# A new pace table for attention's blocks beside the units of a Strassen-like product: more in the first and last unit of each round, fewer in the units between

## The chip, the cores and the metric

The kernel runs on one core of one Trainium2 chip, as one program in one launch. The metric is the device time of that program in microseconds (us). Five engines run side by side, each through its own list of instructions in order: TensorE (PE, matrix products), VectorE (DVE), ScalarE (ACT), GpSimd (POOL) and SyncE (SP). SP issues nearly all DMA transfers, POOL the rest. An engine that must wait for another holds up everything that stands behind the waiting instruction on its own list.

## What is computed

Two independent layers, whose outputs of 2048 x 1024 float32 each are set side by side:

```python
def _A_ref(x, wqkv, wo):
    H = 32; Dh = D // H; W = 256
    qkv = (x @ wqkv).reshape(B, S, 3, H, Dh).transpose(2, 0, 3, 1, 4)
    q, k, v = qkv[0], qkv[1], qkv[2]
    scores = jnp.einsum("bhqd,bhkd->bhqk", q, k) * (Dh ** -0.5)
    mask = (idx[:, None] - idx[None, :] >= 0) & (idx[:, None] - idx[None, :] < W)
    p = _softmax(jnp.where(mask[None, None], scores, -1e9), axis=-1)
    o = jnp.einsum("bhqk,bhkd->bhqd", p, v)
    return o.transpose(0, 2, 1, 3).reshape(B, S, D) @ wo

def _B_ref(x, dft_seq_re, dft_seq_im, dft_hid_re, dft_hid_im):
    a = jnp.einsum("bsd,ed->bse", x, dft_hid_re)
    b = jnp.einsum("bsd,ed->bse", x, dft_hid_im)
    return jnp.einsum("ts,bse->bte", dft_seq_re, a) - jnp.einsum("ts,bse->bte", dft_seq_im, b)

return jnp.concatenate([_A_ref(...), _B_ref(...)], axis=-1)
```

S is 2048, D is 1024. The first is attention of 32 heads in a sliding window of 256 keys; the second is four plain products with cosine and sine matrices that come in as inputs.

## The kernel before

Every float32 operand is split into a float16 high part and a float16 rest, and each product is made of three products of parts. The work comes in four stretches.

*Projections* (to 566 us). A list `order` names 96 pieces of q, k and v, each 24 products of 128 x 512. Between them preparations run for what follows.

*Units* (566 to 1570 us). The second layer's products, 48 units of the helper `seven`, each a 2 x 2 block product with seven multiplications in place of eight: seven positions of twelve products, 84 in all. They use three PSUM banks, a, b and c, in the sequence a b a c a b a; at each position's end ACT or DVE empties the bank just filled (lines 1032, 1034 and 1066), and PE comes back to it one or two positions later. A round has twelve units: four of kind "x" (names `p1_...`, product with the hidden matrix), whose left operand was split beforehand and is loaded ready-made (`x_left`: `un_a`, `un_b`, `un_c` and a part in `reg`), and eight of kind "c" (`p2_...`, product with the sequence matrix), for each of which `u_step` splits a raw tile one unit ahead on ACT and DVE. So during the last unit of a round and the first three of the next no raw tile is split, while the ready-made operands are loaded (for the first unit of a round during the last one of the round before). There are four rounds; units are counted from 0, so rounds begin at units 0, 12, 24 and 36. A "c" unit makes two output tiles. In round 0 SP stores them; from round 1 on they are added to what lies in memory by four accumulating stores per unit, issued by POOL in the unit after (`store`, line 1125).

*Attention* runs beside the projections and the units, as a Python generator that puts its steps between their products. One block is a pair of heads by 128 queries; there are 256. A block's steps: on PE its scores into `s` and `far` (`s_step`); on DVE a masked copy (line 254) and the row maximum (256); on ACT the bias (259), two exponentials (266) and the float16 copy `hl` (269); on DVE the rest of that copy (270); on SP a transposing DMA from `hl` into `t` (272); on POOL two triangular selections (`z_step`, 284 and 286), which stand behind a `mark` that follows a later block's bias; six blocks later on PE the product with v (`v_step`) and on DVE its sum (318). After four blocks `o_step` normalizes, and SP transposes the result (`ot`, line 335) and stores it into `ots` (354). Tile `hl` has three buffers, `s` three banks, `t` six. A block's q, k and v are loaded by SP for four blocks at a time (`qk` line 222, `vt` line 228), about three blocks ahead.

*Tail* (from 1570 us): the output projection, eight units `po0` to `po7`, with nothing of attention left.

How many blocks stand beside which products is set by `tick`: after every four products it adds `4 * rate` to an account, and each whole point is half a block. The rate of a unit is twice a number from the tables `FIRST` (for the four "x" units of a round) and `SECOND` (for its eight "c" units), over 84, so the number is the unit's blocks. Whatever the tables leave of the 256 blocks goes to the projections: `early` is the rest, spread with the weights `EARLY`. At the fifth "c" unit of round 3 everything left is issued at once.

PE's products keep the order in which they are written, and so do ACT's and DVE's instructions where an explicit dependence says so; elsewhere the framework's scheduler orders the instructions of each engine by its own estimate.

The lines that the tables act on:

```python
def tick(n):
    ...
    acc[0] += n * rate[0]
    while acc[0] >= 1.0:
...
early = (NG * NCH * 2 * QB + LAG - in_units) / sum(EARLY.values())
...
rate[0] = 2 * early * EARLY.get(n, 0.85) / 24
...
rate[0] = 2 * ((FIRST if kind == "x" else SECOND)[2 * p + c] + (0,) * 8)[i] / 84
```

Of the kernel before, what the change touches and what calls it, by code (L numbers as in the profile page):

```python
# [53 lines left out]
def fused_kernel(ctx: ExitStack, tc: tile.TileContext, xa, wqk, wv, wo, xb, wd, cs, out):  # L54
# [342 lines left out]
    def at(n, f, *args):  # L397
# [2 lines left out]

    START = 24
    LAST = 4
    FIRST = ((6.6, 4.8, 4.4, 0.6), (4.4, 4.8, 4.8, 0.6), (3.7, 4.9, 4.9, 0.6), (3.7, 5.2, 4.9, 0.6))
    SECOND = ((2.4, 5.0, 5.0, 5.0, 5.0, 5.0, 5.0, 6.2), (2.0, 4.6, 4.6, 4.6, 4.6, 4.2, 4.2, 3.9),
              (2.0, 4.6, 4.6, 4.6, 4.6, 5.0, 5.0, 3.9), (2.0, 4.6, 4.6, 4.6))
    EARLY = {n: (1.0, 0.75, 0.9, 1.05, 1.15, 1.15)[(n - START) // 12] for n in range(START, len(order))}
    in_units = sum(sum(a) for a in FIRST + SECOND) - 0.4 * SECOND[3][LAST - 1]
    early = (NG * NCH * 2 * QB + LAG - in_units) / sum(EARLY.values())
# [677 lines left out]
    with tc.tile_pool(name="pb", bufs=1) as pb:  # L1086
# [45 lines left out]
        for n, (kind, p, c, i) in enumerate(units):  # L1132
            rate[0] = 2 * ((FIRST if kind == "x" else SECOND)[2 * p + c] + (0,) * 8)[i] / 84
            if kind == "x":
# [109 lines left out]
```

## Time and profile before

| | us |
|---|---|
| three runs | 1717.8, 1725.38, 1728.74 |
| their median | 1725.38 |
| the profiled execution | 1720.77 |
| its span, from the first to the last instruction | 1719.0 |
| idle time of PE within the span (1719.0 less 1697.8 busy) | 21.2 |
| DVE busy in the span | 1301.7 |
| ACT busy in the span | 1170.4 |

The granted clock of PE is 0.999 of its full value over the span. A product's own duration in the profile is longer than the time to the next one's start, since products overlap in the array; busy time counts the union. A row of the grouped view names line, engine, operation and operands, then busy time, mean nanoseconds of one, and the idle time of its engine just before it with what ended it. A row of the timeline has the start, the time, and in square brackets the idle time before it and its releaser. A row of the view by stretch gives, for each engine, the busy time and the number of instructions, then the granted clock, the DMA share (the mean busy share of 16 DMA engines; transfers that overlap on one engine both count, so it can pass 1) and GB/s. "SPq" are the DMA instructions on SP's list.

### The profile page before, as it was taken

The page shows a single profiled execution, that of the slowest core. Times are in us where ns is not written, and L with a number is a line of the kernel's source. Part 1 is how long each engine was busy: PE and PEld are TensorE (multiplying, and loading weights), DVE is VectorE, ACT ScalarE, POOL GpSimd, SP SyncE. Part 2 cuts the span into 40 slices and gives each one's busy share as a digit, 9 for nine tenths or more (in the row PEclk, how much of TensorE's full clock was granted, in tenths as well). Part 3 has the DMA queues.
Part 4 walks back from the last instruction along what each step waited for, and adds up shares of the span by engine and source line. Part 5 has one row for each costly group of instructions (what it writes and reads, how often), then busy time and mean ns, then how long its engine had stood idle before and what let it go on. Part 6 is the DMA issues. An engine that isn't in the chain of part 4 may idle for free.

```text
span 1719.0 us, 30875 instructions
## 1 busy us (share of the span) xinstructions
PE 1697.8 (99%) x10999; PEld 852.8 (50%) x10999; DVE 1301.7 (76%) x2225; ACT 1170.4 (68%) x2035; POOL 574.5 (33%) x874
## 2 busy tenths in 40 slices
PE   9999999999999999999999999999999999999999
PEld 4444555554555554555544545555545545444444
DVE  6847788887987788887688786688886688687542
ACT  4466666676876787887787876678876687563322
POOL 0001322444434432444423564433555424411000
PEclk9999999999999999999999999999999999999999
DMA  9747999999998985887998999986999976875431
GB/s 348 246 136 243 252 292 285 270 262 294 250 243 198 212 221 126 206 191 192 235 252 221 189 168 173 224 209 119 193 170 182 214 203 130 169 186 115 119 98 74
DMA packets 469899, 348.63 MB, mean 203 GB/s; under 512 B 376944, under 2 KB 409968, under 8 KB 468848
## 3 DMA queue, kind: packets, MB, share of 16 engines
q1 hardware_dynamic: 462064, 321.48, 74.8%
q0 software_dynamic: 7680, 25.17, 9.2%
q8 instruction: 86, 1.41, 0.3%
q14 instruction: 69, 0.57, 0.1%
HBM read 166.99 MB, written 106.17 MB: 159 GB/s over the span
## 4 chain that ended last, share of the span: by engine, by line
PE 71%; DVE 11%; ACT 7%; DMA 5%; issue 4%; POOL 2%; SPq 0%; DVEq 0%; ACTq 0%; POOLq 0%
PE p_a L114 17%; PE pv L114 13%; PE pk L114 9%; PE p_b L114 8%; PE pq L114 8%; PE po_a L114 5%; PE p_c L114 4%; PE po_b L114 2%; DMA t<-hl 2%; PE s L114 2%; DVE reg L834 1%; DVE hl L270 1%; DVE y L1034 1%; PE po_c L114 1%; ACT s L266 1%
## 5 line engine op out<-in xcount | busy, mean ns | idle before, releaser
L266 ACT ACTIVATE s<-s,bias,escs 128x256 f32<-128x256 f32 (+1 forms) x512 | 270.0, 528 | 11.7
L284 POOL TENSOR_SCALAR_AFFINE_SELECT z<-t 128x512 f16<-128x512 f16 x224 | 185.3, 835 | 189.4 <-PE pv L114 143.0
L270 DVE TENSOR_TENSOR hl<-s,hl 128x512 f16<-128x512 f32 (+1 forms) x256 | 170.2, 665 | 60.9 <-ACT hl L269 60.0
L259 ACT ACTIVATE bias<-mx,pshift,escs 128x2 f32<-128x2 f32 x256 | 98.1, 383 | 164.1 <-DVE mx L256 163.7
L114 PEld LDWEIGHTS <-reg 128*128 128x128 f16 x1344 | 129.1, 98 | 141.5
L286 POOL TENSOR_SCALAR_AFFINE_SELECT t<-t 128x512 f16<-128x512 f16 x224 | 182.9, 825 | 11.4
L114 PE MATMUL p_a<-reg,un_c 128*128 128x512 f16 x768 | 182.9, 381 | 1.1 <-ACT y L1032 0.9
L114 PE MATMUL pk<-reg,wu_k 128*128 128x512 f16 x768 | 174.4, 379 | 0.0
L256 DVE TENSOR_REDUCE mx<-s 128x2 f32<-128x512 f32 (+1 forms) x256 | 170.9, 668 | 3.4
L114 PE MATMUL pv<-reg,reg 128*128 128x512 f16 x768 | 172.7, 379 | 0.0
L114 PEld LDWEIGHTS <-un_c 128*128 128x128 f16 x1152 | 110.3, 98 | 124.7 <-issue 6.5
L263 POOL TENSOR_SCALAR mark<-bias 128x1 f32<-128x1 f32 x128 | 53.0, 414 | 353.3 <-ACT bias L259 352.9
L114 PEld LDWEIGHTS <-un_a 128*128 128x128 f16 x1152 | 109.8, 97 | 122.1 <-issue 6.7
L114 PEld LDWEIGHTS <-un_b 128*128 128x128 f16 x1152 | 110.1, 97 | 121.4 <-issue 5.5
L269 ACT ACTIVATE hl<-s 128x512 f16<-128x512 f32 (+1 forms) x256 | 148.8, 581 | 17.0 <-DMA t<-hl 11.4
L114 PE MATMUL pq<-reg,wu_q 128*128 128x512 f16 x672 | 151.3, 379 | 0.8 <-DVE reg L121 0.5
L114 PE MATMUL p_a<-reg,un_a 128*128 128x512 f16 x576 | 136.2, 379 | 4.4 <-DVE y L1034 4.2
L114 PE MATMUL p_b<-reg,un_b 128*128 128x512 f16 x576 | 136.7, 379 | 1.9 <-DVE reg L834 1.9
L114 PE MATMUL p_a<-reg,un_b 128*128 128x512 f16 x576 | 136.4, 379 | 1.8 <-DVE y L1034 1.6
L114 PE MATMUL p_c<-reg,un_a 128*128 128x512 f16 x576 | 136.5, 379 | 0.0
L254 DVE COPY_PREDICATED s<-upper,far 128x256 f32<-128x256 uint32 x224 | 94.5, 422 | 49.4 <-PE s L114 47.9
L114 PEld LDWEIGHTS <-qk 96*128 96x128 f16 x1056 | 87.9, 97 | 65.7 <-issue 2.6
(208 smaller groups left out, 3154.2 us busy)
## 6 DMA issues: line engine op xcount, KB each, us to landing
raw_u<-in_cs_dram SPq DMA_DIRECT2D x64, 512.0 KB, 4.9
qk<-qk SPq DMA_DIRECT2D x64, 384.0 KB, 4.9
out_dram<-y POOLq DMA_DIRECT2D x72, 256.0 KB, 6.2
raw_wd<-in_wd_dram SPq DMA_DIRECT2D x24, 512.0 KB, 5.3
vs<-yv SPq DMA_DIRECT2D x32, 264.0 KB, 4.4
vt<-vs SPq DMA_DIRECT2D x64, 132.0 KB, 4.4
raw_wo<-in_wo_dram SPq DMA_DIRECT2D x16, 512.0 KB, 7.4
qk<-yq SPq DMA_DIRECT2D x32, 256.0 KB, 3.2
```

The costliest lines, as they stand in the source:

```text
L114: fixed[:] = [nc.tensor.matmul(*args, **kwargs)]
L254: nc.vector.copy_predicated(s[:, :, P:], upper2, d["far"] if nb == 3 else never2)
L256: nc.vector.tensor_reduce(mx, sv, axis=AX.X, op=ALU.max, negate=True)
L259: nc.scalar.activation(bias, mx, AF.Identity, bias=pshift, scale=es)
L263: marks[:] = [nc.gpsimd.tensor_scalar(mark, bias[:, 0:1], 1.0, None, op0=ALU.mult)]
L266: nc.scalar.activation(sv[:, h], sv[:, h], AF.Exp, bias=bias[:, h:h + 1], scale=es)
L269: nc.scalar.activation(hi, sv, AF.Copy)
L270: behind[:] = [nc.vector.tensor_tensor(lo, sv, hi, op=ALU.subtract)]
L284: nc.gpsimd.affine_select(out=z, in_=pk, compare_op=ALU.is_gt, fill=0.0, base=0, pattern=[[0, 4], [-1, P]], channel_multiplier=1)
L286: nc.gpsimd.affine_select(out=pk, in_=pk, compare_op=ALU.is_ge, fill=0.0, base=0, pattern=[[0, 4], [1, P]], channel_multiplier=-1)
L834: nc.vector.tensor_tensor(lo, src, hi, op=ALU.subtract)
L1034: slice(None), [nc.vector.scalar_tensor_tensor(y, ps, f, y, op0=ALU.mult, op1=ALU.add)])
```

## The change

Two tables of numbers are replaced; nothing else is touched.

```diff
-    FIRST = ((6.6, 4.8, 4.4, 0.6), (4.4, 4.8, 4.8, 0.6), (3.7, 4.9, 4.9, 0.6), (3.7, 5.2, 4.9, 0.6))
-    SECOND = ((2.4, 5.0, 5.0, 5.0, 5.0, 5.0, 5.0, 6.2), (2.0, 4.6, 4.6, 4.6, 4.6, 4.2, 4.2, 3.9),
-              (2.0, 4.6, 4.6, 4.6, 4.6, 5.0, 5.0, 3.9), (2.0, 4.6, 4.6, 4.6))
+    FIRST = ((7.4, 4.8, 4.4, 0.6), (6.6, 4.7, 4.6, 0.6), (6.4, 4.8, 4.7, 0.6), (6.4, 5.0, 4.7, 0.6))
+    SECOND = ((1.6, 4.3, 4.3, 4.3, 4.3, 4.3, 4.3, 6.6), (1.6, 3.9, 3.9, 3.9, 3.9, 3.9, 3.9, 6.4),
+              (1.6, 3.9, 3.9, 3.9, 3.9, 3.9, 3.9, 6.4), (1.6, 4.2, 4.2, 4.2))
```

Counted in the built order by the blocks whose scores PE makes in each unit, before and now:

| round | first unit | next four | six in the middle | last unit |
|---|---|---|---|---|
| 0 (units 0 to 11) | 7, now 8 | 12, now 11 | 30, now 26 | 6, now 7 |
| 1 (12 to 23) | 5, now 6 | 12, now 12 | 27, now 23 | 3, now 7 |
| 2 (24 to 35) | 4, now 6 | 13, now 12 | 28, now 23 | 4, now 6 |
| 3 (36 to 47) | 4, now 7 | 12, now 12 | 7, now 6 | 0, now 0 |

The projections get 84 blocks for 82. The sum is 256 in both.

The first place is SP's list at the border of rounds 1 and 2, from the loads of unit 24's last operands (`un24_b`, `un24_c`) to unit 25's first (`un25_a`). In the names, `t_181` is block 181's transposed tile. Before:

```order
L272 DMA_TRANSPOSE t_181_13349<-hl_181_13346 128x8x128
L786 DMA un24_b_13400<-xs_60 128x2048
L786 DMA un24_c_13436<-xs_60 128x2048
L272 DMA_TRANSPOSE t_182_13393<-hl_182_13390 128x8x128
L781 DMA reg1_83<-xs_60 128x1024
L786 DMA un25_a_13521<-xs_60 128x2048
```

Now:

```order
L786 DMA un24_b_13326<-xs_60 128x2048
L272 DMA_TRANSPOSE t_179_13285<-hl_179_13282 128x8x128
L228 DMA vt_5_1_2_13403<-vs_58 128x4x132
L786 DMA un24_c_13394<-xs_60 128x2048
L272 DMA_TRANSPOSE t_180_13319<-hl_180_13316 128x8x128
L335 DMA_TRANSPOSE ot_5_0_3_13364<-ohl_5_0_3_13361 128x4x128
L222 DMA qk_5_1_2_13401<-qk_57 96x2048
L781 DMA reg1_83<-xs_60 128x1024
L354 DMA ots_59<-ot_5_0_3_13364 128x512
L272 DMA_TRANSPOSE t_181_13391<-hl_181_13388 128x8x128
L786 DMA un25_a_13502<-xs_60 128x2048
```

Between the load of `un24_b` and that of `un25_a` stood one block's transpose; now three stand there, with a transpose and a store of an `ot`.

The second place is DVE's list in unit 32, in the middle of round 2, from the first instruction after the last step on the raw tile of unit 33 to the instruction that empties bank a of unit 32 (line 1034, `p2_32_a`). Before:

```order
L254 COPY_PREDICATED s_216_15754<-upper_90,far_1026 128x2x128
L121 TENSOR_REDUCE top1_u34_15747<-top_u34_15668 128x1
L256 TENSOR_REDUCE mx_216_15762<-s_216_15754 128x2
L270 TENSOR_TENSOR hl_215_15718<-s_215_15704,hl_215_15718 128x512
L318 TENSOR_REDUCE o_6_1_0_15676<-pv_210_15789 128x132
L121 SCALAR_TENSOR_TENSOR un33_c_15782<-raw_u33_1_15117,sc_u33_15622,un33_c_15782 128x1024
L327 RECIPROCAL rs_6_1_0_15815<-o_6_1_0_15676 128x8
L1034 SCALAR_TENSOR_TENSOR y2_6765<-p2_32_a_15632,fu32_15348,y2_6765 128x512
```

Now:

```order
L254 COPY_PREDICATED s_215_15742<-upper_90,far_1026 128x2x128
L256 TENSOR_REDUCE mx_215_15748<-s_215_15742 128x2
L121 SCALAR_TENSOR_TENSOR un33_c_15762<-raw_u33_1_15134,sc_u33_15599,un33_c_15762 128x1024
L270 TENSOR_TENSOR hl_214_15689<-s_214_15677,hl_214_15689 128x512
L1034 SCALAR_TENSOR_TENSOR y2_6835<-p2_32_a_15609,fu32_15331,y2_6835 128x512
```

Ahead of the emptying of the bank stood five instructions of attention (lines 254, 256, 270, 318 and 327, of blocks 215 and 216 and of an earlier block's sum); now three do.

The third place is SP's list in the projections, at the load of q and k for blocks 48 to 51 (`qk_1_1_0`). Before:

```order
L272 DMA_TRANSPOSE t_43_4285<-hl_43_4282 128x8x128
L887 DMA qk_57<-yq4_3_4390 128x512
L272 DMA_TRANSPOSE t_44_4332<-hl_44_4329 128x8x128
L886 DMA qk_57<-yq4_3_4390 128x2x512
L335 DMA_TRANSPOSE ot_1_0_1_4374<-ohl_1_0_1_4371 128x4x128
L222 DMA qk_1_1_0_4446<-qk_57 96x2048
```

Now:

```order
L272 DMA_TRANSPOSE t_43_4247<-hl_43_4244 128x8x128
L886 DMA qk_57<-yq4_2_4355 128x2x512
L222 DMA qk_1_1_0_4401<-qk_57 96x2048
L648 DMA wx_114<-in_wd_dram 128x1024
L939 DMA wds_61<-wx_114 256x1x1024
L335 DMA_TRANSPOSE ot_1_0_1_4347<-ohl_1_0_1_4344 128x4x128
L272 DMA_TRANSPOSE t_44_4297<-hl_44_4294 128x8x128
```

The load stood behind block 44's transpose and that of `ot_1_0_1`; now it stands ahead of both.

## Prediction

> **What bounds the kernel now.** I read the head of the page first, to see which engine fills the span.
>
> ```profile
> span 1719.0 us, 30875 instructions
> PE 1697.8 (99%) x10999; PEld 852.8 (50%) x10999; DVE 1301.7 (76%) x2225; ACT 1170.4 (68%) x2035; POOL 574.5 (33%) x874
> ```
>
> TensorE (PE) is busy all but 21.2 us. The change moves attention's blocks and neither adds nor removes a product, so those 21.2 us, with what slow products cost, are all that can be won. The second view is the busy time by stretch, cut at the first product of a unit: units 1 to 4, the middle of round 0 (units 5 to 10), units 11 and 12, then the same four kinds again: 13 to 16, middle 17 to 22, 23 and 24, 25 to 28, middle 29 to 34, 35 and 36, 37 to 40.
>
> ```profile
> core 0: us, PE busy (x) PEld busy (x) DVE busy (x) ACT busy (x) POOL busy (x), PEclk, DMA share, GB/s
> 588.50:670.00 81.50, 81.00 (x536) 40.66 (x533) 71.65 (x122) 63.97 (x116) 25.82 (x37) 1.00 0.70 173
> 670.00:798.20 128.20, 128.12 (x969) 67.85 (x968) 111.02 (x207) 110.14 (x202) 58.49 (x85) 1.00 0.81 189
> 798.20:841.80 43.60, 43.60 (x352) 23.50 (x351) 26.12 (x48) 30.06 (x59) 15.61 (x29) 1.00 1.04 245
> 841.80:924.50 82.70, 80.72 (x521) 40.26 (x519) 70.70 (x125) 64.13 (x114) 26.08 (x34) 1.00 0.93 256
> 924.50:1056.70 132.20, 128.50 (x921) 66.43 (x920) 106.59 (x187) 101.75 (x188) 72.48 (x99) 0.99 0.98 169
> 1056.70:1097.60 40.90, 40.90 (x285) 20.89 (x283) 20.02 (x36) 22.39 (x43) 16.82 (x26) 1.00 1.09 217
> 1097.60:1178.90 81.30, 80.83 (x526) 40.62 (x525) 70.83 (x124) 64.55 (x116) 27.94 (x37) 1.00 0.77 177
> 1178.90:1309.20 130.30, 127.60 (x952) 67.07 (x950) 109.94 (x196) 105.50 (x192) 75.82 (x101) 1.00 0.98 174
> 1309.20:1350.40 41.20, 41.20 (x289) 21.16 (x288) 20.84 (x36) 24.39 (x48) 19.39 (x31) 1.00 1.04 213
> 1350.40:1434.30 83.90, 81.64 (x547) 40.86 (x545) 72.50 (x124) 64.96 (x116) 25.37 (x36) 1.00 0.79 180
> ```
>
> Length less PE's busy time is its idle time. The middles of rounds 1 and 2 lose 3.70 and 2.70 us; the middle of round 0, with more blocks but no accumulating stores, 0.08. The stretches of units 1 to 4, 13 to 16, 25 to 28 and 37 to 40 lose 0.50, 1.98, 0.47 and 2.26. The last and first units lose nothing, and there VectorE (DVE) is busy 49% and 51% in rounds 1 to 3, against 81% and 84% in the middles. But their DMA share, 1.09 and 1.04, is the highest of all. Third, I looked at what ends the two longest idle times of the middles.
>
> ```profile
> 1257.58 2.75 PE L114 MATMUL p_b<-reg 128*128 128x512 f16 x12
> 1262.04 1.24 PE L114 MATMUL p_a<-reg,un_b 128*128 128x512 f16 x5 [1.59 <-DVE y L1034]
> ...
> 1023.98 0.22 PE L114 MATMUL far<-qk 96*128 96x128 f16 x1 [1.38 <-DVE s L254]
> 1025.33 4.44 PE L114 MATMUL p_a<-reg,un_c 128*128 128x512 f16 x12 [0.85 <-ACT y L1032]
> ...
> 1022.27 0.60 ACT L269 ACTIVATE hl<-s 128x512 f16<-128x512 f32 x1 [5.17 <-DMA t<-hl]
> 1257.45 0.60 ACT L269 ACTIVATE hl<-s 128x512 f16<-128x512 f32 x1 [4.02 <-DMA t<-hl]
> ...
> 1242.82 4.74 SPq L272 DMA_TRANSPOSE t<-hl  x1
> 1247.65 1.22 SPq L335 DMA_TRANSPOSE ot<-ohl  x1
> 1257.79 0.33 SPq L354 DMA_DIRECT2D ots<-ot  x1
> 1258.22 3.94 SPq L272 DMA_TRANSPOSE t<-hl  x3
> ```
>
> PE waits for a PSUM bank that DVE or ScalarE (ACT) empties, but both were late because ACT stood 5.17 and 4.02 us in front of a copy into `hl`. That tile has three buffers, and one is free when its transposing DMA has landed. At 1247.65 SyncE (SP) issued the transpose of `ot`, and the store of it in the next row went out only at 1257.79, once `ot` had landed; three `t` transposes stood behind it. So the bound is PE, and what breaks it are late transposes, by way of `hl`.
>
> **Part 1: fewer blocks in the middles.** By the order, the middles of rounds 1 and 2 go from 27 and 28 blocks to 23 each, that of round 0 from 30 to 26. One block costs ACT and DVE this much:
>
> ```profile
> L266 ACT ACTIVATE s<-s,bias,escs 128x256 f32<-128x256 f32 (+1 forms) x512 | 270.0, 528 | 11.7
> L270 DVE TENSOR_TENSOR hl<-s,hl 128x512 f16<-128x512 f32 (+1 forms) x256 | 170.2, 665 | 60.9 <-ACT hl L269 60.0
> L259 ACT ACTIVATE bias<-mx,pshift,escs 128x2 f32<-128x2 f32 x256 | 98.1, 383 | 164.1 <-DVE mx L256 163.7
> L256 DVE TENSOR_REDUCE mx<-s 128x2 f32<-128x512 f32 (+1 forms) x256 | 170.9, 668 | 3.4
> L269 ACT ACTIVATE hl<-s 128x512 f16<-128x512 f32 (+1 forms) x256 | 148.8, 581 | 17.0 <-DMA t<-hl 11.4
> L254 DVE COPY_PREDICATED s<-upper,far 128x256 f32<-128x256 uint32 x224 | 94.5, 422 | 49.4 <-PE s L114 47.9
> ```
>
> DVE 0.665 + 0.668 + 0.422 = 1.76 us, ACT 2 x 0.528 + 0.383 + 0.581 = 2.02 us. Five blocks fewer in a middle of 130 us take 8.8 us from DVE, from 84% to about 80%, and the three buffers of `hl` last one fifth longer. Idle time to win: 3.70 + 2.70 = 6.4 us. To it comes a slow stretch: the twelve products at 1025.33 took 4.44 us where twelve at 1257.58 took 2.75, so 1.69 us more, right behind two idle times of 1.38 and 0.85. Together 8.1 us. It can win at most this, and lose a little if the new order makes other collisions: -8.1 to +2. The cause is a DMA's landing, which thinner blocks ease without removing; I take 70%, -5.7. The middle of round 0 has 0.08 to give: nothing.
>
> The Trainium skill (TensorE: Matmul & The Clock Gate, section "Why this matters for your kernels") asks for no idle gaps of over about 3 us if throughput isn't to drop. By that rule the 1.69 us aren't the work of the two gaps, and the sum would be 0.7 x 6.4 = 4.5 us won in place of 5.7. The row speaks against it here, with gaps of half that size and less, and I go by the row.
>
> **Part 2: more blocks in the last and first units.** The pair 23 and 24 goes from 7 blocks to 13, 35 and 36 from 8 to 13, 11 and 12 from 11 to 13. PE's time for them only moves. Engines: six blocks more give DVE 20.02 + 6 x 1.76 = 30.6 us and ACT 22.39 + 6 x 2.02 = 34.5, in a pair that PE's own work makes longer: 168 products of (2.75 - 0.38) / 11 = 0.215 us (0.38 is one product's own time) are 36.2 us, and with 11 blocks the pair took 43.6, so 0.67 us a block and 44.9 us with 13. That is 68% and 77%. POOL's part of a block:
>
> ```profile
> L284 POOL TENSOR_SCALAR_AFFINE_SELECT z<-t 128x512 f16<-128x512 f16 x224 | 185.3, 835 | 189.4 <-PE pv L114 143.0
> L286 POOL TENSOR_SCALAR_AFFINE_SELECT t<-t 128x512 f16<-128x512 f16 x224 | 182.9, 825 | 11.4
> ```
>
> Six times 0.835 + 0.825 on 16.82 are 26.8 us, 60%; the four stores that POOL issues in each of these units stand behind marks, which come closer together now. So these three engines hide it. Each block also brings a transpose to SP's queue, and every fourth block two loads, the transpose of `ot` and its store, between the loads of the next unit's weights. The transposes may not be hidden:
>
> ```profile
> L272 SPq DMA_TRANSPOSE t<-hl x11: 1237/1522/2924, 800.7 to 837.0; - x11
> DMA to landing us min/median/max: 3.0/5.2/7.5
> ...
> L272 SPq DMA_TRANSPOSE t<-hl x8: 1319/1616/4258, 1058.7 to 1094.9; - x8
> DMA to landing us min/median/max: 4.2/7.0/8.5
> ...
> L272 SPq DMA_TRANSPOSE t<-hl x8: 1237/1682/3722, 1310.8 to 1348.3; - x8
> DMA to landing us min/median/max: 2.8/7.5/9.7
> ```
>
> These are the pairs 11/12 (no POOL stores), 23/24 and 35/36. A buffer of `hl` is held for 0.58 (ACT) + 0.67 (DVE) + a place in SP's queue (about one transpose, 1.6) + 7.0 to 7.5 to the landing, some 10 us. Three buffers give one block each 3.3 us. The new pace is 44.9 / 13 = 3.45 us, and in a last unit of seven blocks (84 x 0.215 + 7 x 0.67) / 7 = 3.25. So the loop is just at its limit there, where before (pace 40.9 / 7 = 5.8) it had room. If the medians hold, only the late ones cost: a landing of 9.7 makes the loop 12.6, 2.9 us past three blocks at 3.25. I take one such wait per pair, less half a us that the banks give: 2.5 us each, +5 in all for two pairs. Lower end 0, as in the pair 11/12 with eleven blocks and no idle time. Upper end: at 10 us the loop takes 12.85 us, 4.28 a block, 0.83 over the pace; 13 blocks, two pairs: +22, and +3.4 if each pair meets a slow stretch of 1.69. The pair 11/12 gets two blocks more at a landing of 5.2: nothing, up to +2.
>
> **Part 3: units 1 to 4, 13 to 16, 25 to 28, 37 to 40.** They keep 12, 12, 13, 12 blocks as 11, 12, 12, 12. Their idle 5.2 us stand in units in which round products, not blocks, load DVE: I take 0, between -3 and +3.
>
> **Part 4: before the units.** Two blocks more, 84 for 82, are 3.5 us of DVE, spread over all the projections: nothing. One wait there is on the path:
>
> ```profile
> L114 PE MATMUL s<-qk 96*128 96x256 f16 (+1 forms) x512 | 105.7, 258 | 1.7 <-DMA qk<-qk 1.7
> ```
>
> It falls on block 48, whose load stands behind the `ot` transpose and block 44's on SP. In the new order it stands ahead of both. I take -1.5, between -1.7 and +1 (another load may be late next).
>
> **Sum.** -5.7 + 5 + 0 - 1.5 = -2.2 us. The profiled execution took 1720.8 us (span 1719.0 and 1.8 around it), so 1718.6 by its own measure. The median of the three runs, 1725.4, lies 4.6 above it: 1723.2 by that. The single execution and the three runs bear about equally on what a new median will be: I say 1721.
>
> **Rivals.** First, the other sign: the `hl` loop becomes the bound of the two pairs. For it speaks the DMA share, at its peak there already and about to take five and six more blocks' transposes; against it, that the pair 11/12 ran eleven blocks without idle time, though without POOL's stores. It decides when the landing's median in the pairs passes 7.8 us, since then (0.58 + 0.67 + 1.6 + 7.8) / 3 = 3.55 is 0.1 over the pace, and 26 x 0.1 with the two late ones of part 2 is the 7.2 us that parts 1 and 4 win. At 10 us: +25.4 - 7.2 = +18, 1739 by its own measure, 1744 by the median. Second, all waits of the middles and block 48 go and no new one comes: -8.1 - 1.7, and -3 from part 3: 1708 by its own measure, 1713 by the median. For it speaks that the middle of round 0 lost 0.08 us with five blocks a unit; against it, that this middle has no accumulating stores. Third, the waits merely change their places, since stores and loads stay where they are and an `ot` that lands late stops SP at any pace: 1721 to 1725.
>
> **Chances and range.** Forecast (own time within 8 us of the profiled one) 0.55; the loop as bound 0.24, half of it beyond +1%; all waits gone 0.13; only moved 0.08. About 1% is what a measurement of this kernel can tell from no change: 1708 and 1743 from the median. Faster than that needs the second rival and a low measurement: 0.06. Slower: 0.12. Within: 0.82. The range reaches from just past the second rival's end to the middle of the first one's, 1707 to 1740; the forecast's own is 1713 to 1731.
>
> **What would show it.** Part 1: idle time of PE in units 17 to 22 and 29 to 34 down from 6.4 to about 2 us, and ACT's waits for `t<-hl` there shorter. Part 2: landing of `t` near 7 to 8 us in units 23/24 and 35/36, one or two waits of ACT for `hl` there, DVE at about 70%. Part 4: no wait for `qk` near 413 us. I am wrong if PE idles over 10 us in the two pairs, or if the middles keep their 6 us though they have fewer blocks.

## The result, and the profile after

The changed kernel takes 1737.62 us (median of 7 runs, 1733.87 to 1741.92) against 1720.48 for the kernel before, run beside it (7 runs, 1713.81 to 1728.74): a ratio of 1.0109, 95% interval 1.0085 to 1.0132. It is slower by 17 us, where 1721 was forecast. Its profiled execution took 1734.69 us, 13.9 more than the one profiled before. The head of its page:

```profile
span 1732.9 us, 30890 instructions
PE 1698.7 (98%) x10999; PEld 852.8 (49%) x10999; DVE 1303.9 (75%) x2225; ACT 1170.8 (68%) x2035; POOL 560.2 (32%) x874
```

The products are the same. PE's busy time grew by 0.9 us, its idle time from 21.2 to 34.2: of these 13.9 us 13.0 are waiting. The view by stretch of the changed kernel, cut as in the prediction (projections, units 1 to 4, middle of round 0, units 11 and 12, then 13 to 16, middle, 23 and 24, 25 to 28, middle, 35 and 36, 37 to 40, and last 44 to 47; the columns are those of the view in the prediction). "The three pairs" are from here on units 11/12, 23/24 and 35/36, a last unit with the first one of the next round:

```profile
141.00:572.00 431.00, 427.14 (x2967) 220.00 (x2965) 353.17 (x624) 302.50 (x542) 149.56 (x274) 1.00 1.00 260
595.10:678.90 83.80, 80.41 (x516) 39.85 (x515) 71.10 (x119) 64.42 (x114) 22.04 (x32) 1.00 0.73 169
678.90:804.70 125.80, 125.80 (x918) 65.84 (x917) 104.33 (x190) 101.18 (x182) 47.87 (x72) 1.00 0.75 178
804.70:850.20 45.50, 44.41 (x365) 23.98 (x362) 29.20 (x56) 33.25 (x66) 19.63 (x35) 1.00 1.02 222
850.20:931.30 81.10, 80.46 (x520) 40.20 (x519) 71.38 (x125) 64.36 (x115) 23.11 (x35) 1.00 0.93 266
931.30:1055.40 124.10, 124.10 (x880) 64.20 (x879) 100.38 (x175) 95.86 (x170) 69.12 (x88) 1.00 0.93 173
1055.40:1102.60 47.20, 44.68 (x363) 24.02 (x361) 26.93 (x52) 31.57 (x64) 24.03 (x39) 1.00 0.99 204
1102.60:1188.00 85.40, 80.90 (x519) 40.30 (x519) 73.30 (x129) 65.08 (x117) 25.71 (x37) 1.00 0.77 176
1188.00:1313.80 125.80, 124.52 (x881) 64.31 (x880) 101.19 (x175) 95.79 (x171) 66.71 (x89) 1.00 0.88 166
1313.80:1360.30 46.50, 44.56 (x361) 23.98 (x358) 26.63 (x52) 32.21 (x65) 23.87 (x39) 1.00 1.10 220
1360.30:1445.70 85.40, 81.06 (x521) 40.32 (x520) 72.74 (x129) 65.28 (x117) 25.84 (x39) 1.00 0.74 174
1506.40:1583.30 76.90, 73.32 (x340) 33.09 (x338) 62.86 (x80) 45.09 (x56) 12.41 (x16) 1.00 0.73 162
```

Of the kernel before, the same view for the two stretches that the prediction did not show (projections, units 44 to 47):

```profile
141.00:566.40 425.40, 423.67 (x2933) 218.32 (x2932) 347.86 (x617) 300.06 (x532) 152.98 (x268) 1.00 0.99 260
1495.70:1569.90 74.20, 73.22 (x340) 33.14 (x339) 61.87 (x75) 44.88 (x56) 12.10 (x16) 1.00 0.70 167
```

Length less PE's busy time, before and after: the middles of rounds 1 and 2 went from 6.4 us to 1.3, the three pairs from 0 to 1.09 + 2.52 + 1.94 = 5.6. But the units behind the pairs and at the rounds' starts, whose numbers of blocks barely change, went from 0.5 to 3.4 (1 to 4), from 0.5 to 4.5 (25 to 28) and from 2.3 to 4.3 (37 to 40), with 13 to 16 going from 2.0 to 0.6; the projections from 1.7 to 3.9; units 44 to 47, where no block is left, from 1.0 to 3.6.

How a wait comes about there shows in the timeline of the changed kernel, in unit 24 and in unit 37 (start, time, instruction, in brackets the idle time before it and its releaser):

```profile
1084.85 4.11 SPq L272 DMA_TRANSPOSE t<-hl  x2
1088.30 0.63 POOL L284 TENSOR_SCALAR_AFFINE_SELECT z<-t 128x512 f16<-128x512 f16 x1 [5.71 <-DMA t<-hl]
1089.60 0.61 POOL L329 TENSOR_TENSOR o<-o,rs 128x256 f32<-128x256 f32 x1
1090.25 0.49 ACT L332 ACTIVATE ohl<-o 128x256 f16<-128x256 f32 x1 [4.17 <-POOL o L329]
...
1092.68 1.02 PE L114 MATMUL p_a<-wx,un_c 128*128 128x512 f16 x4 [1.38 <-ACT y L1032]
...
1364.86 0.60 ACT L269 ACTIVATE hl<-s 128x512 f16<-128x512 f32 x1 [4.50 <-DMA t<-hl]
...
1366.09 1.89 PE L114 MATMUL p_b<-reg,un_b 128*128 128x512 f16 x8 [2.66 <-ACT y L1032]
```

In unit 37 it is the way that the prediction knew: a transpose lands late, ACT stands 4.50 us for a buffer of `hl`, the emptying of a bank (line 1032) stands behind it, and PE waits 2.66. In unit 24 it is a second way: POOL stands 5.71 us for the transposed tile, its multiplication of `o` (line 329) stands behind that, ACT stands 4.17 for `o`, and again the emptying of a bank behind it. Not every wait of the pairs comes that way. Two of them end with the load of a later block's q and k (line 222), 1.09 and 0.85 of the 5.6 us:

```profile
830.60 0.23 PE L114 MATMUL far<-qk,qk 96*128 96x128 f16 x1 [1.09 <-DMA qk<-qk]
...
1081.89 0.23 PE L114 MATMUL far<-qk,qk 96*128 96x128 f16 x1 [0.85 <-DMA qk<-qk]
```

### The profile page after: what moved, and what is told of

It is laid out like the page before. It is cut to its first block, busy times and chain, and to the rows that moved or that the text cites. A ratio compares the mean times of both kernels' runs of the same rounds, so it can differ in the third digit from the quotient of the medians.

```text
span 1732.9 us, 30890 instructions
## 1 busy us (share of the span) xinstructions
PE 1698.7 (98%) x10999; PEld 852.8 (49%) x10999; DVE 1303.9 (75%) x2225; ACT 1170.8 (68%) x2035; POOL 560.2 (32%) x874
## 3 DMA queue, kind: packets, MB, share of 16 engines
q0 software_dynamic: 7680, 25.17, 9.0%
## 4 chain that ended last, share of the span: by engine, by line
PE 77%; DVE 8%; DMA 7%; ACT 4%; issue 2%; POOL 1%; SPq 0%; DVEq 0%; ACTq 0%; POOLq 0%
PE p_a L114 20%; PE pv L114 13%; PE p_b L114 10%; PE pq L114 9%; PE pk L114 8%; PE p_c L114 5%; PE po_a L114 5%; DMA raw_u<-in_cs_dram 3%; DMA t<-hl 3%; PE s L114 2%; PE po_b L114 2%; DVE reg L834 1%; PE far L114 1%; PE po_c L114 1%; DMA qk<-qk 1%
## 5 line engine op out<-in xcount | busy, mean ns | idle before, releaser
L284 POOL TENSOR_SCALAR_AFFINE_SELECT z<-t 128x512 f16<-128x512 f16 x224 | 170.6, 765 | 221.3 <-PE pv L114 167.9
L263 POOL TENSOR_SCALAR mark<-bias 128x1 f32<-128x1 f32 x128 | 49.3, 385 | 344.5 <-ACT bias L259 343.8
L269 ACT ACTIVATE hl<-s 128x512 f16<-128x512 f32 (+1 forms) x256 | 148.7, 581 | 16.9 <-DMA t<-hl 12.2
```

The lines of the kernel that those rows point to most:

```text
L263: marks[:] = [nc.gpsimd.tensor_scalar(mark, bias[:, 0:1], 1.0, None, op0=ALU.mult)]
L269: nc.scalar.activation(hi, sv, AF.Copy)
L284: nc.gpsimd.affine_select(out=z, in_=pk, compare_op=ALU.is_gt, fill=0.0, base=0, pattern=[[0, 4], [-1, P]], channel_multiplier=1)
```

## The experiments

The idle time of PE by stretch in every kernel, each number a length less PE's busy time as above, from one profiled execution. The first column names the runs of the sections below. Between the changed kernel and its repetition single stretches differ by up to 1.7 us, and units 37 to 40 by 3.9 between the kernel before and `one_round_in_place`, which have the same blocks there. So a difference in a single row proves little; what is read is what comes again in several rows.

| kernel | projections | 1–4 | three middles | three pairs | 13–16 | 25–28 | 37–40 | 44–47 | whole span |
|---|---|---|---|---|---|---|---|---|---|
| before | 1.7 | 0.5 | 6.5 | 0.0 | 2.0 | 0.5 | 2.3 | 1.0 | 21.2 |
| changed | 3.9 | 3.4 | 1.3 | 5.6 | 0.6 | 4.5 | 4.3 | 3.6 | 34.2 |
| after_again | 4.2 | 1.7 | 0.0 | 4.6 | 1.1 | 5.2 | 3.6 | 3.5 | 31.1 |
| mid_only | 11.6 | 2.1 | 1.0 | 0.0 | 2.0 | 5.3 | 2.5 | 4.1 | 38.0 |
| pairs_only | 0.0 | 0.0 | 3.0 | 5.9 | 8.5 | 5.2 | 0.3 | 2.1 | 31.8 |
| store_later | 4.7 | 2.1 | 1.4 | 3.2 | 1.5 | 5.7 | 1.8 | 2.8 | 29.6 |
| shift_before | 3.7 | 3.6 | 3.4 | 0.0 | 1.8 | 6.0 | 0.3 | 1.0 | 26.5 |
| shift_after | 0.0 | 3.0 | 0.0 | 4.3 | 2.8 | 5.4 | 4.3 | 1.0 | 31.0 |
| o_on_vector | 5.4 | 1.7 | 1.2 | 5.1 | 1.6 | 8.1 | 6.1 | 2.2 | 38.2 |
| no_adding_stores | 5.1 | 2.7 | 0.0 | 1.9 | 0.6 | 1.9 | 0.4 | 1.0 | 20.1 |
| plain_stores | 5.1 | 2.8 | 0.0 | 0.3 | 0.8 | 4.5 | 0.4 | 1.0 | 22.1 |
| before_no_adding_stores | 1.6 | 0.5 | 0.1 | 0.0 | 1.9 | 0.3 | 0.8 | 1.0 | 13.3 |
| shift_before_other_way | 0.0 | 0.1 | 2.6 | 0.0 | 2.5 | 2.5 | 2.3 | 1.0 | 17.7 |
| before_store_later | 1.6 | 0.0 | 3.8 | 0.0 | 2.0 | 0.3 | 0.2 | 1.0 | 15.8 |
| one_round_in_place | 2.3 | 0.9 | 3.2 | 0.0 | 2.1 | 3.7 | 6.2 | 1.0 | 26.1 |
| two_rounds_in_place | 2.4 | 0.1 | 0.1 | 3.7 | 2.1 | 3.8 | 2.9 | 1.0 | 23.2 |
| two_rounds_store_later | 1.2 | 0.7 | 0.1 | 1.0 | 2.1 | 3.4 | 0.2 | 1.0 | 16.8 |

### The change again, and its two halves

The changed kernel unaltered:

> The changed kernel once more, for a second profile of it. Theory (too dense a pace in the last and first units makes transposes late, and the units behind inherit the backlog): PE idles 4 to 8 us in the three pairs of a last and a first unit and 8 to 13 us in units 1 to 4, 25 to 28 and 37 to 40 again, within 3 us of the first profile (5.6 and 12.2). Rival (one execution's chance): these stretches change places with others, and less than half of it comes again. The 3.6 us of units 44 to 47, which have no attention, are chance by both: between 1 and 4.

It took 1736.56 us, ratio 1.0112 (1.0084 to 1.0140): the loss is the change's own. Units 1 to 4, 25 to 28 and 37 to 40 idle 10.5 us again for 12.2, and units 44 to 47 idle 3.5 again: those waits are not the chance that the expectation took them for. Then the new middles with the old last and first units, which puts 98 blocks into the projections:

```diff
-    FIRST = ((7.4, 4.8, 4.4, 0.6), (6.6, 4.7, 4.6, 0.6), (6.4, 4.8, 4.7, 0.6), (6.4, 5.0, 4.7, 0.6))
-    SECOND = ((1.6, 4.3, 4.3, 4.3, 4.3, 4.3, 4.3, 6.6), (1.6, 3.9, 3.9, 3.9, 3.9, 3.9, 3.9, 6.4),
-              (1.6, 3.9, 3.9, 3.9, 3.9, 3.9, 3.9, 6.4), (1.6, 4.2, 4.2, 4.2))
+    FIRST = ((6.6, 4.8, 4.4, 0.6), (4.4, 4.8, 4.8, 0.6), (3.7, 4.9, 4.9, 0.6), (3.7, 5.2, 4.9, 0.6))
+    SECOND = ((1.6, 4.3, 4.3, 4.3, 4.3, 4.3, 4.3, 6.2), (1.6, 3.9, 3.9, 3.9, 3.9, 3.9, 3.9, 3.9),
+              (1.6, 3.9, 3.9, 3.9, 3.9, 3.9, 3.9, 3.9), (1.6, 4.2, 4.2, 4.2))
```

> The new numbers for the middles alone, the old ones for the last and first units; the 14 blocks so freed go to the projections (98 blocks in place of 84). Theory: the pairs idle under 1 us and the units behind them 3 to 6 as before, the middles under 1.5: 7 us under the kernel before by these stretches, and the projections pay for 14 more blocks with 0 to 10 us of new waits; in all 1712 to 1724. Rival (the loss sits in the projections' pace, not in the pairs): the projections lose over 10 us and the total is at or over the changed kernel's.

And the new last and first units with the old middles, 68 blocks in the projections:

```diff
-    SECOND = ((1.6, 4.3, 4.3, 4.3, 4.3, 4.3, 4.3, 6.6), (1.6, 3.9, 3.9, 3.9, 3.9, 3.9, 3.9, 6.4),
-              (1.6, 3.9, 3.9, 3.9, 3.9, 3.9, 3.9, 6.4), (1.6, 4.2, 4.2, 4.2))
+    SECOND = ((2.4, 5.0, 5.0, 5.0, 5.0, 5.0, 5.0, 6.6), (2.0, 4.6, 4.6, 4.6, 4.6, 4.2, 4.2, 6.4),
+              (2.0, 4.6, 4.6, 4.6, 4.6, 5.0, 5.0, 6.4), (2.0, 4.6, 4.6, 4.6))
```

> The new numbers for the last and first units alone, the old ones between; 14 blocks fewer in the projections (68). Theory: the pairs and the units behind them lose 12 to 20 us, the middles 5 to 8 as before: 1732 to 1745, no better than the changed kernel. Rival (the projections' pace is what costs): the projections lose 3 us or less and the total is at or under the kernel before.

Middles alone took 1745.92 us (ratio 1.0168, 1.0140 to 1.0196), which is the rival's outcome; pairs alone 1741.21 (1.0131, 1.0109 to 1.0153), the theory's. Neither half is faster than both together, and neither can be read as a term of a sum: the blocks that a half takes away go to the projections or come from there. With 98 blocks those lose 11.6 us. The middles and pairs themselves did about as the theory had it (1.0 and 0.0 us in the first kernel; 5.9 for the pairs in the second, though its middles lost 3.0 for the 5 to 8 expected). But units 25 to 28 lost 5.3 us behind a pair of the old density, which a backlog from dense pairs does not explain.

### The store of `ot` behind a later transpose

```diff
-                    nc.sync.dma_start(*store_o.pop(0))
+                    with tc.issue_after(line[0].ins):
+                        nc.sync.dma_start(*store_o.pop(0))
```

> The changed kernel, with the store of ot ordered behind a transpose three or four blocks later, so that SP doesn't stand still until ot has landed. If SP's standing still is what makes the transposes late: the wait of SP for ot falls from some 130 us to under 20, PE's idle time in the pairs and in units 1 to 4, 25 to 28, 37 to 40 falls from 17.8 to under 10 us, and the total by 6 us or more. Rival (DMA engines too busy, the queue only mirrors it): the wait for ot goes, the landing of t gets as much longer, PE's idle time stays within 4 us.

It took 1731.88 us (ratio 1.0082, 1.0060 to 1.0104), some 5 us less than the change, and left 12.8 of the 17.8 us of idle time, between the two outcomes. SyncE's own waits (line, what for, us in all, times, longest), in the changed kernel

```profile
SPq L354 <- DMA ot<-ohl: 108.8, 53, 5.1
```

and with the later store

```profile
SPq L335 <- DMA ots<-ot: 54.0, 33, 4.9
```

show that half of the time in which SP's list stood was moved, not removed: the next transpose of `ot` now waits for the store before it. It helps, and is a part of the time only. Nor is that wait what the change added: in the kernel before SP's list stood 130.2 us for `ot`, longer than in the changed one.

### Place of the blocks

Two kernels leave every unit up to 40 its number of blocks and change only the last three, so that all blocks of units 1 to 40 shift against the units' own work. First the kernel before, by 0.84 of a block:

```diff
-              (2.0, 4.6, 4.6, 4.6, 4.6, 5.0, 5.0, 3.9), (2.0, 4.6, 4.6, 4.6))
+              (2.0, 4.6, 4.6, 4.6, 4.6, 5.0, 5.0, 3.9), (2.0, 4.9, 4.9, 5.0))
```

> The old numbers of blocks in every unit up to 40; only the last three units get 0.84 of a block more in all, so that every block of units 1 to 40 comes 0.84 of a block earlier or later against the units' own work, and the projections run 76.1 blocks for 76.9. Theory A (the dense pairs leave late transposes behind, whatever the place): nothing dense is new, so the time stays within 3 us of before and units 13 to 16, 25 to 28 and 37 to 40 keep some 5 us of PE's idle time. Theory B (the loss behind the pairs comes from where the blocks' steps fall in the units' own work): the old place of the blocks was the good one, so 8 us or more above before, and idle time in units 25 to 28 of 3 us or more for 0.5.

Then the changed kernel, by 2.4 blocks:

```diff
-              (1.6, 3.9, 3.9, 3.9, 3.9, 3.9, 3.9, 6.4), (1.6, 4.2, 4.2, 4.2))
+              (1.6, 3.9, 3.9, 3.9, 3.9, 3.9, 3.9, 6.4), (1.9, 5.0, 5.0, 5.0))
```

> The new numbers in every unit up to 40, and 2.4 blocks taken from the projections to the last three units: unit 13 begins at block 135.2 for 137.6, unit 25 at 182.9 (as in the kernel before) for 185.3, unit 37 at 230.8 for 233.2; the projections run 77.4 blocks for 79.8. Theory A: pairs and the units behind them lose as in the changed kernel (17.8 us of idle time), only the projections may win 0 to 3: 1733 to 1738. Theory B: units 25 to 28 and 37 to 40 fall from 4.5 and 4.3 us of idle time to about 2 each: 1727 to 1731.

The old pace, shifted, took 1732.85 us: ratio 1.0086 (1.0054 to 1.0117), nearly the whole loss of the change without a dense pair or a thin middle. (Its profiled execution, 1725.26 us, was its fastest, so the rows show less than the median.) Its view by stretch, projections, units 1 to 4, units 25 to 28:

```profile
141.00:568.50 427.50, 423.78 (x2929) 218.04 (x2928) 347.83 (x613) 299.23 (x531) 143.97 (x265) 1.00 0.98 259
590.60:675.20 84.60, 80.97 (x533) 40.60 (x532) 72.67 (x126) 64.88 (x117) 25.18 (x37) 1.00 0.72 168
1099.70:1188.60 88.90, 82.92 (x525) 40.92 (x524) 72.77 (x125) 63.67 (x114) 22.89 (x34) 0.98 0.71 167
```

Idle: 3.7, 3.6 and 6.0 us, with 0.8 of a block fewer in the projections and not one more in units 1 to 40. So theory B held here. The longest of these waits is in unit 27, and SyncE's list shows it. In the kernel before, the load of the last half of unit 29's raw tile (line 208) is issued ahead of the store of `ot`:

```profile
1144.02 0.58 SPq L208 DMA_DIRECT2D raw_u<-in_cs_dram  x1
...
1146.64 0.33 SPq L354 DMA_DIRECT2D ots<-ot  x1
```

In the shifted kernel it stands behind that store and one more transpose, some 9 us later, 7 as the units go (unit 25 begins at 1097.6 and at 1099.7):

```profile
1149.27 1.19 SPq L335 DMA_TRANSPOSE ot<-ohl  x1
1151.69 0.33 SPq L354 DMA_DIRECT2D ots<-ot  x1
1152.11 1.23 SPq L272 DMA_TRANSPOSE t<-hl  x1
1153.40 0.58 SPq L208 DMA_DIRECT2D raw_u<-in_cs_dram  x1
...
1158.43 1.06 ACT L761 ACTIVATE junk<-raw_u 128x1024 uint8<-128x1024 f32 x1 [4.56 <-DMA raw_u<-in_cs_dram]
...
1163.62 1.86 PE L114 MATMUL p_a<-wx,un_c 128*128 128x512 f16 x4 [3.47 <-DVE y L1034]
```

ACT stands 4.56 us for the tile, all steps on it come late, and DVE empties the bank late. No transpose is late for its own reader here: what the place decides is which of the unit's loads stand behind a step that waits in SyncE's list. The code makes this so: the helper `load` (lines 206 to 208) orders its DMA behind the one written last on a list that block transposes share. What a load without this order would take was not tried.

For the changed kernel the time came out as theory B had it, 1729.19 us (1.0074, 1.0048 to 1.0100), but not by its way. The projections idle 0.0 us at 77.4 blocks for 3.9, and units 44 to 47 lose 1.0 for 3.6; but units 25 to 28, which now begin at block 182.9 as before the change, still lose 5.4 and 37 to 40 still 4.3, as theory A had it. The middles, with all their old blocks, fell to 3.4 us of idle time in the shifted old kernel: they too hung on the place, not on the number alone.

The old kernel shifted half a block the other way:

```diff
-              (2.0, 4.6, 4.6, 4.6, 4.6, 5.0, 5.0, 3.9), (2.0, 4.6, 4.6, 4.6))
+              (2.0, 4.6, 4.6, 4.6, 4.6, 5.0, 5.0, 3.9), (2.0, 4.4, 4.4, 4.4))
```

> The old numbers up to unit 40, half a block (0.52) taken from the last three units and given to the projections, so that every block of units 1 to 40 stands half a block the other way than in the first shift. If the old place of the blocks is the good one against any move: 1723 to 1735, with 2 us or more of new idle time in at least two of the stretches projections, 1 to 4, 25 to 28. If the first shift only met a bad place: 1714 to 1721.

1716.94 us, ratio 0.9985 (0.9966 to 1.0003): no loss. So not any move costs; the first shift met a bad place.

### POOL's queue

```diff
-            nc.gpsimd.tensor_tensor(on, on, rs.unsqueeze(2).to_broadcast([P, 2 * QB, DH]), op=ALU.mult)
+            nc.vector.tensor_tensor(on, on, rs.unsqueeze(2).to_broadcast([P, 2 * QB, DH]), op=ALU.mult)
```

> The changed kernel with the multiplication of o (64 in all, 0.695 us each on POOL) moved to VectorE, so that ScalarE's copy into ohl no longer waits for what stands ahead in POOL's queue. If POOL's queue is the way by which late transposes reach ScalarE: its waits on POOL for ohl, 31.8 us in all, fall to under 3, and the time by 5 to 10 us, 1727 to 1732. If the hl buffers are the way: within 3 us of 1737, with the waits on t<-hl as long as before (12 to 19 us). VectorE gets some 30 us more work, so a rise above 1740 would show that its queue is worth more than POOL's.

No gain: 1741.17 us (1.0138, 1.0112 to 1.0164), beside the changed kernel's 1.0109. What ended ACT's idle time before line 269, first in the changed kernel, then here (us, times):

```profile
  DMA t<-hl: 12.2, 6
```

```profile
  DMA t<-hl: 28.8, 15
```

The waits on POOL for `ohl` went, and those for `t<-hl` more than doubled. So taking the link out of POOL's queue wins nothing. Whether the 64 multiplications on DVE cost what the link had cost is not shown.

### The adding stores

The 96 stores that add the later rounds into the second half of the output were left out, of the changed kernel and of the one before; the output lacks those additions. The same edit to both:

```diff
-                        do(n + 1, (0 if t % 2 else 4) + 2 * half, store, dst[rows], src[rows])
+                        pass
```

> The changed kernel without the 96 adding stores that POOL issues; left out is the sum of the later rounds into the second half of the output. If those stores' load on the DMA engines is what makes the transposes land late: landing of t in the pairs 23/24 and 35/36 from a median of 5.2 and 6.2 us to about 4, idle time behind them to under 2 us each, and 12 to 20 us faster, 1717 to 1725. If the transposes themselves and SyncE's queue make them late: 1730 to 1736 with waits for t<-hl as before.

> The kernel before without the 96 adding stores; left out is the sum of the later rounds into the second half of the output. Theory A (the stores' load costs both kernels, and the new pace adds to it): the idle time of rounds 1 to 3, some 11 us and as much as 17 with slow products, falls to about 3, 1702 to 1709; then the changed kernel without stores (1714.9) is still 6 to 12 us behind, by its projections, units 1 to 4 and 44 to 47. Theory B (stores hurt only where blocks are dense): 1714 to 1719, and the two kernels are equal without stores.

Changed without them: 1714.89 us, ratio 0.9987 (0.9971 to 1.0003). Before without them: 1710.92, 0.9946 (0.9931 to 0.9962). The stores cost the kernel before 0.5% and the changed kernel 1.2%; without them the two kernels stand 1714.89 - 1710.92 = 4.0 us apart by their medians and 0.4%, some 7 us, by the ratios, each run having its own kernel before beside it; with them 17. So theory A of the second expectation held in kind: both kernels gain, the one before 9 us, and a difference is left. The stretches of units 23 and 24, 25 to 28, 35 and 36, 37 to 40 in the changed kernel without stores:

```profile
1056.40:1100.50 44.10, 44.10 (x361) 23.97 (x358) 28.37 (x55) 32.50 (x65) 19.03 (x35) 1.00 0.86 198
1100.50:1182.90 82.40, 80.53 (x521) 40.33 (x520) 71.99 (x125) 63.84 (x114) 21.48 (x34) 1.00 0.71 164
1307.00:1351.10 44.10, 44.10 (x362) 23.98 (x359) 28.02 (x54) 32.01 (x65) 17.67 (x33) 1.00 0.89 192
1351.10:1431.90 80.80, 80.42 (x521) 40.33 (x520) 71.88 (x125) 65.12 (x116) 24.44 (x38) 1.00 0.72 168
```

The four lost 13.3 us in the changed kernel (2.5, 4.5, 1.9, 4.3) and lose 2.3 here at the same order of blocks; units 44 to 47 are back at 1.0. Projections, units 1 to 4 and the pair 11/12, which lie ahead of the first adding store, keep their waits. The transposes land sooner. For line 272 in the pairs 23/24 and 35/36, with the stores

```profile
DMA to landing us min/median/max: 2.4/5.2/7.1
...
DMA to landing us min/median/max: 2.7/6.2/7.8
```

and without

```profile
DMA to landing us min/median/max: 2.3/3.6/6.2
...
DMA to landing us min/median/max: 2.7/4.1/7.8
```

Is it the bytes or the adding? The same 96 stores as plain ones, the additions left out:

```diff
-                nc.gpsimd.dma_start(dst, src, accum_op=ALU.add)
+                nc.gpsimd.dma_start(dst, src)
```

> The changed kernel with the 96 stores as plain ones; left out is the addition to what the second half of the output held, so that no old value is read. If it is the reading and adding that holds the DMA engines and makes the transposes late: half or more of the 22 us that no stores won, 1717 to 1727. If the bytes and the packets of any store do it: 1731 to 1738 and waits as in the changed kernel.

1721.17 us, ratio 0.9997 (0.9977 to 1.0018). By the ratios, leaving the stores out won 1.2% (21 us) and making them plain 1.1% (19 us). The adding is most of it; only units 25 to 28 keep 4.5 us. What the adding holds up is not parted further: beside the DMA engines (last section) POOL gains too, since a store takes a median of 0.55 us of its list for 0.90.

### Dense pairs, all else in its old place

The new pace in units 16 to 24 alone, with the middle set so that every block outside keeps its place:

```diff
-    FIRST = ((6.6, 4.8, 4.4, 0.6), (4.4, 4.8, 4.8, 0.6), (3.7, 4.9, 4.9, 0.6), (3.7, 5.2, 4.9, 0.6))
-    SECOND = ((2.4, 5.0, 5.0, 5.0, 5.0, 5.0, 5.0, 6.2), (2.0, 4.6, 4.6, 4.6, 4.6, 4.2, 4.2, 3.9),
+    FIRST = ((6.6, 4.8, 4.4, 0.6), (4.4, 4.8, 4.8, 0.6), (6.4, 4.9, 4.9, 0.6), (3.7, 5.2, 4.9, 0.6))
+    SECOND = ((2.4, 5.0, 5.0, 5.0, 5.0, 5.0, 5.0, 6.2), (1.6, 3.7, 3.7, 3.7, 3.7, 3.6, 3.6, 6.4),
```

> The kernel before with the new pace in units 17 to 24 alone (middle of round 1 at 3.7 and 3.6, the pair 23/24 at 6.4 each), summed so that every block outside them keeps its old place. Both theories: the middle of round 1 gives back its 3.7 us of idle time (6.5 with the slow products), the pair loses 0.5 to 2.6. Backlog (the dense pair leaves late transposes): units 25 to 28 lose 4 us or more for 0.5, and the time stays within 3 us of before. Place: units 25 to 28 keep 1 us or less, and it is 3 to 6 us faster, 1712 to 1717.

Its middle, pair and units 25 to 28:

```profile
926.30:1049.60 123.30, 123.30 (x856) 63.42 (x854) 100.13 (x176) 93.50 (x166) 66.52 (x86) 1.00 0.93 164
1049.60:1093.50 43.90, 43.90 (x353) 23.77 (x352) 26.55 (x50) 31.65 (x64) 24.61 (x40) 1.00 1.08 237
1093.50:1180.20 86.70, 83.04 (x526) 41.07 (x525) 73.16 (x129) 64.99 (x117) 29.18 (x37) 0.98 0.75 175
```

The middle gives back its 3.7 us, the pair itself loses nothing, and the units behind lose 3.7 for 0.5, at a granted clock of 0.98. The time is 1723.16 us, ratio 1.0011 (0.9990 to 1.0031): the backlog's outcome. This execution alone would not prove it, since units 37 to 40 lost 6.2 us in it, though every block is back in its old place from unit 25 on: such a wait also comes and goes by itself. Unit 25, directly behind the pair, does over all seventeen traces. PE idles 1.0 to 3.9 us there in each of the ten kernels with a dense pair 23/24 and the stores, adding or plain, and 0.0 in the six with the old pair and in the changed kernel without stores. In this run it is one wait of 2.52 us at 1108.22: POOL stood 3.59 us for a transposed tile, ACT 1.85 for the `o` that stood behind that, and only then emptied the bank. In the changed kernel unit 25 makes 2.3 of the 4.5 us of units 25 to 28. Unit 28 makes another 1.7, which are the same with plain stores and with none; with the blocks in their old place, as in this run, it is 0.3. So this part is place.

The same in rounds 1 and 2, with this on top:

```diff
-    FIRST = ((6.6, 4.8, 4.4, 0.6), (4.4, 4.8, 4.8, 0.6), (6.4, 4.9, 4.9, 0.6), (3.7, 5.2, 4.9, 0.6))
+    FIRST = ((6.6, 4.8, 4.4, 0.6), (4.4, 4.8, 4.8, 0.6), (6.4, 4.9, 4.9, 0.6), (6.4, 5.2, 4.9, 0.6))
-              (2.0, 4.6, 4.6, 4.6, 4.6, 5.0, 5.0, 3.9), (2.0, 4.6, 4.6, 4.6))
+              (1.6, 3.9, 3.9, 3.9, 3.9, 4.0, 4.0, 6.4), (2.0, 4.6, 4.6, 4.6))
```

> The same in rounds 1 and 2: the middles of both thin, the pairs 23/24 and 35/36 dense, all else in its old place. Backlog: units 25 to 28 and 37 to 40 lose 4 us each (for 0.5 and 2.3), and with 2 us in each pair the time is 1717 to 1723. Place: those units lose 0.5 and 2.3 as before, the middles give back 6.4 us and the pairs take 2 to 5: 1711 to 1717.

1722.28 us, ratio 1.0001 (0.9980 to 1.0022). The middles lose 0.1 us in all for 6.5; the pairs take 3.7 and units 25 to 28 3.3 more: what the middles won is given back.

### A version that beats both

The later store in the kernel before, and in the one with two rounds in place:

> The kernel before with the store of ot issued behind a later transpose of t, as in the run with that edit on the changed kernel, where it won some 5 us. If late transposes and SyncE's wait for ot lengthen each other at any pace: 3 to 8 us faster than before, 1710 to 1715, and the middles' 6.4 us of idle time fall to about 3. If the kernel before owes its time to the place of each step, and any move costs: 1718 to 1730.

> Two rounds in place, and the store of ot behind a later transpose. If what the pairs and the units behind them lose is SyncE's wait for ot: idle time there under 2 us in all, and below the kernel before with the later store, 1706 to 1712. If it is the adding stores on the DMA engines: 1712 to 1718, with the pairs' and the following units' idle time as in the run without the later store.

1713.08 us, ratio 0.9969 (0.9952 to 0.9986), and 1713.28, ratio 0.9956 (0.9932 to 0.9980), each beside its own runs of before. Both beat the kernel before and the changed one; between them there is nothing to tell. The first came out as expected if late transposes and the wait for `ot` lengthen each other (the middles at 3.8 us, for about 3). In the second the pairs fall to 1.0 and units 37 to 40 to 0.2, but units 25 to 28 keep 3.4 us behind the dense pair, later store or not: the time is that of the second outcome, the waits fit neither.

## Why the prediction was wrong, step by step

**Part 1 held, its cause only in part.** Forecast -5.7 us; the middles gave 5.2 of idle time and the 1.69 of slow products. The step read the store of `ot` and the three transposes behind it as what made the wait at 1257.45. But they went out at 1257.79 and 1258.22, when that wait was over; it ended with a transpose issued before `ot`, at 1242.82, which took 14.5 us to land. But the old number of blocks lost 3.4 us after a mere shift for 6.5, and 0.1 without the adding stores. Thinner blocks are one of several ways out of that collision.

**Part 2 held in its number, its cause only in part.** Forecast +5 for two pairs, with the third at nothing; they lost 2.5 and 1.9, and the third 1.1. The landing's median was 5.2 and 6.2 us, not 7.0 to 7.5, so the loop of `hl` had more room than assumed, (0.58 + 0.67 + 1.6 + 6.2) / 3 = 3.0 us a block for a pace of 3.45; DVE was busy 57% in both pairs, not 68. The step's own way, ACT standing for a buffer of `hl`, shows in the pair 35/36 (3.9 us of such waits) and not in 23/24, where POOL's queue and a load of q and k took its place; the load makes all of 11/12. That the sum fits is partly luck. (The rival's threshold was added up wrong: 26 x 0.1 and the two late waits of 2.5 us are 7.6, not 7.2.)

**Part 3 failed.** "I take 0" for units 1 to 4, 13 to 16, 25 to 28 and 37 to 40: in the order of these stretches they came to 2.9 - 1.3 + 4.0 + 2.1 = +7.7 us of idle time. The step looked at their numbers of blocks, which stay, and not at what else sets a wait there: what the dense pair leaves on the DMA engines (one round in place: 3.2 us behind one pair; unit 25 in ten traces), and the place of each block's steps among the unit's own (a shift alone: +3.1 in units 1 to 4 and +5.5 in 25 to 28). The first comes by way of late transposes and needs the stores, adding or plain, of which the prediction had said only that they stand behind marks. The second comes, in the one wait that was followed, by way of a load that SyncE issues late; the waits of units 1 to 4 were not followed so far.

**Part 4 failed.** Forecast -1.5 with two blocks more at no cost; it came to +2.1 of idle time and 1.7 of slow products. The load for block 48 went out ahead of both transposes, as the order says, and PE waited for it all the same. Three rows of the changed kernel's timeline:

```profile
408.04 0.29 PE L114 MATMUL s<-qk 96*128 96x128 f16 x2 [1.11 <-DMA qk<-qk]
...
425.04 0.22 PE L114 MATMUL far<-qk 96*128 96x128 f16 x1 [2.74 <-DVE s L254]
...
425.37 5.30 PE L114 MATMUL pq<-reg,wu_q 128*128 128x512 f16 x16
```

1.11 us at 408.04 for the 1.7 of before, and then a new wait of 2.74 for DVE's masked copy; the next sixteen products took 5.30 us, where at part 2's 0.215 us from start to start and 0.38 for the last they take 15 x 0.215 + 0.38 = 3.6. An order shows that a load is issued earlier, not that it is early enough. Nor is it the number of blocks alone. By the account of `tick`, less its six blocks of lag, the projections run 76.9 before and 79.8 in the changed kernel; 77.4 in two other kernels cost nothing, 76.1 cost 3.7.

**A stretch that was left out.** Units 44 to 47 have no blocks and took +2.6, with ACT again waiting for a raw tile. The forecast has no term for them. They are back at 1.0 without the adding stores, with plain ones, and also in both shifted kernels. Which of the stores reach them was not tried. In idle time the terms come to -5.2 + 5.6 + 7.7 + 2.1 + 2.6 = +12.8 of the 13.0 us between the two profiles; the slow products that the middles won came back in the projections.

**The rivals.** The first, the loop of `hl` as the bound of the pairs, gave the nearest time (1739 to 1744) by another mechanism: it asked for a landing of 7.8 us, and the pairs lost 5.6 us, not 25. The others gave times that were too low. What the forecast lacked was a case in which both parts come as worked out and the stretches between them, priced at nothing, pay.

**What stays open.** The change in place costs nothing (1.0001), the whole change 1.1%. The rest comes from the moved place, round 0, unit 36's follow-up and the projections, and was not split further. What makes a place bad has no rule here: two shifts of the old table gave +0.9% and -0.2%. And the profile of the changed kernel flatters it: of its seven runs it has the highest granted clock, 0.999, the others 0.995 to 0.998. So some of the 17 us between the medians, beyond the 13.9 between the profiles, are probably slow products that no row here shows.

## What to carry to other kernels

In a schedule laid out by hand, the stretches whose own numbers stay are not free when the sum ahead of them changes: price them by shifting the old schedule by a part of a step and timing that, ahead of any gain from a new shape. Where PE is 99% busy, look for what makes transfers late (here the adding stores, and loads that stand in a queue behind a wait) rather than for a pace that avoids them: thin and dense stretches only moved the waits. And a queue that stands for a landing, as SyncE did with the store of `ot`, is worth a line of code first: it gave 0.3% to 0.45% in three kernels.

## What the runs showed of the hardware

A store that adds holds the DMA engines much longer than a plain one of the same size. The rows of POOL's queue (packets, MB, share of 16 engines' span), of the changed kernel

```profile
q0 software_dynamic: 7680, 25.17, 9.0%
```

and with plain stores

```profile
q0 software_dynamic: 7680, 25.17, 5.2%
```

come to 0.090 x 16 x 1732.9 / 7680 = 0.325 us a packet, against 0.052 x 16 x 1718.2 / 7680 = 0.186.

PE slows after some short waits, and the granted clock shows which. The sixteen products at 425.37, which lost 1.7 us, follow a gap of 2.74; the eight at 1366.09 follow one of 2.66 and took 1.89 us, which is full pace. In the view by stretch of the changed kernel, around the first gap and around the second, the granted clock is the third number from the end:

```profile
422.95:426.36 3.41, 1.32 (x9) 0.79 (x9) 3.37 (x6) 1.26 (x4) 2.12 (x2) 1.00 1.06 306
426.36:429.77 3.41, 3.41 (x10) 1.18 (x8) 3.06 (x5) 3.38 (x7) 0.00 (x0) 0.50 1.09 377
...
1361.61:1365.03 3.42, 1.82 (x11) 0.90 (x10) 0.00 (x0) 0.17 (x1) 0.13 (x1) 1.00 1.26 138
1365.03:1368.44 3.41, 2.35 (x31) 1.40 (x31) 1.46 (x3) 2.60 (x5) 2.40 (x4) 1.00 1.12 272
```

The clock stood at half for 3.41 us behind the first and not behind the second. In all seventeen traces, the first and last 10 us aside, it stands at half for 3.41 us or twice that, and within a trace these stretches begin whole multiples of 3.41 us apart. Cut into such steps, the clock fell to half behind steps in which PE idled 1.94 us or more, and never behind one with less; between 1.94 and 2.05 both happened. The gap of 2.74 put 3.41 - 1.32 = 2.09 us into one step, that of 2.66 was split into 1.6 and 1.06. The Trainium skill (TensorE: Matmul & The Clock Gate, section "Why this matters for your kernels") puts the bound at about 3 us for a gap; the first gap was shorter, and the trace decides.
